# Attention and gated MLP on one core: pairs of neighbouring units by rows, a ring of six row buffers, output projections one iteration later

## The chip, the core and the metric

The kernel runs on one core of one Trainium2 chip. Such a core has a matrix engine (TensorE, "PE" in the profile, with its weight loads shown apart as "PEld"), a vector engine (VectorE, DVE), an engine for activation functions (ScalarE, ACT), a general engine (GpSimd, POOL) and a queue that mostly issues transfers (SyncE, SP). Sixteen DMA engines serve all queues. The metric is the device time of one execution in microseconds; the time of a version is the median of its runs.

## What is computed

A transformer block with modulation: layernorm and grouped attention with a cached K and V, then layernorm and a gated MLP that mixes along the sequence. There are 2048 rows of width 512, 32 query heads over 8 K/V heads (four query heads share one), 2048 keys and a head width of 128.

```python
def _A_ref(x, k_cache, v_cache, wq, wo):
    q = (x @ wq).reshape(B, Sq, Hq, Dh) ...          # 32 heads
    k, v = repeat of the 8 cached heads, 4 times
    scores = einsum('bhqd,bhkd->bhqk', q, k) * Dh ** (-0.5)
    p = softmax(scores)
    o = einsum('bhqk,bhkd->bhqd', p, v)
    return o.reshape(B, Sq, Hq * Dh) @ wo

def _B_ref(x, w_in, w_sp, b_sp, w_out):
    z = gelu(x @ w_in); z1 = z[..., :Fh]; z2 = layernorm(z[..., Fh:])
    g = einsum('ts,bsf->btf', w_sp, z2) + b_sp
    return (z1 * g) @ w_out

mod = silu(c) @ w_mod                                # sa, ca, ga, sb, cb, gb
h = layernorm(x) * (1 + ca) + sa;  x = x + ga * _A_ref(h, ...)
h = layernorm(x) * (1 + cb) + sb;  x = x + gb * _B_ref(h, ...)
```

## The kernel before

The attention is cut into 128 **units**. A unit is one of the 8 groups (a K/V head with its four query heads) and one of 16 tiles of 128 query rows; unit u belongs to group u // 16. One iteration of the main loop (L1350) computes the scores of unit `it` (`qk`, L986) and, beside them, the product with V of an earlier unit. It is cut into eight **slots**. A slot has two score products of 128x512 and one ScalarE instruction that takes the exponential of both (1024 columns), an eighth of a V product, and mostly one "fill": a step of the query projection for later units (L944; four per unit) or of the output projection (`wo_proj`, L1108; four per unit, in slots 4 to 7).

The order of all instructions is written out by hand: each engine executes its queue in the order in which the program issues, and waits where data or a buffer is missing. `at(it, slot, fn)` puts a step at the start of a slot; `later` and `fill` hold these steps. Loads by POOL's queue run as early as their buffers allow, in the queue's own order, since POOL has little else to do.

A unit is computed in one of two ways:

- **By columns.** The scores come transposed, keys on the partitions (L1020), the exponentials go straight into the buffer `pT` (L1027), and the product with V (`pv`, L1076) takes `pT` as the weights: 64 products of 129 columns, the 129th being the softmax sum. VectorE divides (L1087, L1088), and a DMA transpose on SyncE's queue turns the result into `oT` (L1096).
- **By rows.** The scores have queries on the partitions (L1001), the exponentials go to a row buffer `pn` together with their sums (L1008). `turn_rows` (L1034), two slots after a head is complete, divides the rows on VectorE (L1042) and issues a DMA transpose of 128x2048 into `pT` (L1045), so four per unit. The product with V (`pv_rows`, L1055) has V as the weights: 16 products of 512 columns. `oT` comes out as it is needed, and VectorE copies it (L1064).

`by_rows` (L967) chooses: even units from 8 to 120 go by rows (57 units), all others by columns. `pv_at` (L970) gives the iteration of the V product: u + 3 by rows, u + 1 by columns. The output projection follows two iterations later (L1359). `homes` (L974) hands out three `pT` buffers by when they come free. There are four row buffers, one for each head of a unit (L660): three lie in the tile for the MLP's input weights `win_sb`, and one in `wmod_a`, the first part of the modulation weights, both unused at that time.

The weights of the next group are loaded during a group: query weights `wq_g` at place 7, K at 9 (a DMA transpose from DRAM on SyncE's queue), V at 11, output weights `wo_g` at 13 (L1251 to L1256). `wq_g`, `v1` and `wo_g` have two buffers each and go by POOL's queue, so that a load starts when the last reader of the group before last is done. On the same queue are the layernorm's small operations and the rows `ga_rows` and `gb_rows`, which go out to DRAM and back at iteration 5 (`mod_rows`, L1171).

After the 128 units the MLP runs; its first part overlaps the last iterations, and it is not touched by the change.

Of the kernel before, what the change touches and what calls it, by code (L numbers as in the profile page):

```python
# [10 lines left out]
BF16 = mybir.dt.bfloat16  # L11
# [564 lines left out]
def kernel(  # L576
# [147 lines left out]
    def load_v(g):  # L724
        v1 = late.tile([P, NKT, DV], BF16, name="v1")
        nc.gpsimd.memset(v1[:, :, DH:DV], 1.0)
        if g > 0:
            nc.gpsimd.dma_start(out=v1[:, :, 0:DH], in_=v_dram[:, g])
        else:
            nc.sync.dma_start(out=v1[:, 0 : NKT // 2, 0:DH], in_=v_rows)  # L730
            nc.sync.dma_start(
                out=v1[:, NKT // 2 : NKT, 0:DH], in_=v_dram[:, 0, NKT // 2 : NKT]
            )
        groups[g]["v1"] = v1

# [230 lines left out]

    def by_rows(u):  # L967
        return TURN_A <= u < TURN_B and u % 2 == 0

    def pv_at(u):  # L970
        return u + 3 if by_rows(u) else u + 1


    users, homes = dict(pT0=-2, pT1=-1, wsp=CT + 2), {}  # L974
    for u in range(NU):
        homes[u] = min(users, key=lambda k: users[k])
        assert users[homes[u]] < u
        users[homes[u]] = pv_at(u)
# [7 lines left out]
    def qk(u, i):  # L986
# [10 lines left out]
        if by_rows(u):  # L997
            hh, half = divmod(i, 2)
            for c in range(2):
# [8 lines left out]
            nc.scalar.activation(  # L1008
                out=pn[hh][:, half * HK : (half + 1) * HK],
                in_=s_ps[:],  # L1010
# [21 lines left out]
        )  # L1032

    def turn_rows(u, hh):  # L1034
        c0 = u * REP + hh
        rs, rinv = rsums[u], rall[:, c0 : c0 + 1]
        tot = stat.tile([P, 1], FP32, name="tot")
        nc.vector.tensor_tensor(  # L1038
            out=tot[:], in0=rs[:, 2 * hh : 2 * hh + 1], in1=rs[:, 2 * hh + 1 : 2 * hh + 2], op=ALU.add
        )  # L1040
        nc.vector.reciprocal(out=rinv, in_=tot[:])  # L1041
        nc.vector.tensor_scalar(  # L1042
            out=pn[hh], in0=pn[hh], scalar1=rinv, scalar2=None, op0=ALU.mult
        )
        nc.sync.dma_start_transpose(  # L1045
            out=pTs[u][:, :, hh * P : (hh + 1) * P], in_=pn[hh]
        )

    def pv_rows(u, i, n):
# [12 lines left out]
        if i == n - 1:  # L1062
            oTs[u] = late.tile([P, REP, P], BF16, name="oT", bufs=3)
            nc.vector.tensor_copy(  # L1064
                out=oTs[u][:], in_=o_pss[u][:].rearrange("p (r q) -> p r q", r=REP)
            )

    def pv(u, i):
# [25 lines left out]
        if i == NSLOT - 1:  # L1094
            oTs[u] = late.tile([P, REP, P], BF16, name="oT", bufs=3)
            nc.sync.dma_start_transpose(  # L1096
# [253 lines left out]
    for it in range(NU + 6):  # L1350
# [202 lines left out]
```

## Time and profile before

| | |
|---|---|
| median of three runs | 1315.53 us (1315.16 to 1317.28) |
| the profiled execution's own time | 1315.63 us |
| its span, first to last instruction | 1313.5 us |
| PE busy | 1293.9 us, 99% |
| ACT busy | 1109.7 us, 84% |
| DVE busy | 683.1 us, 52% |
| transfers of SyncE's queue, share of 16 DMA engines' span | 62.3% |
| transfers of POOL's queue | 4.6% |
| V products by columns (L1076) | 4480 of 128x129 |
| V products by rows (L1055) | 912 weight loads of 128x128 |

Stages, by the view of stretches: up to 81.97 us the start and units 0 to 7, up to 116.14 the units 8 to 11 in which the rows begin, up to 1084.84 the alternating units, up to about 1130 the last units by columns, then the MLP to the end.

The busy times are sums over one profiled execution. Matmuls are pipelined and their ends are modelled, so a time per matmul is best read from the distance of two starts; in the timeline the length of one (0.38 us for 512 columns) is more than that distance. An entry in brackets after a line is idle time of the engine before that instruction, and what ended it.

### The profile page before, as it was taken

How to read it: one execution, taken by the hardware profiler on the slowest of the kernel's cores; microseconds unless marked ns; L12 is line 12 of the kernel's file. 1: busy time of each engine (PE TensorE's matmuls, PEld its weight loads, DVE VectorE, ACT ScalarE, POOL GpSimd, SP SyncE). 2: the span in 40 equal slices, each digit the busy share in tenths (PEclk: the TensorE clock that was granted, in tenths of full speed). 3: DMA queues.
4: the chain of work that ended last, by engine and by line, in shares of the span. 5: the costliest groups of instructions: out<-in, count | busy, mean ns of one | idle time of the engine just before them, and what ended most of it. 6: DMA issues, size and time to landing. Idle time of an engine off the chain costs nothing.

```text
span 1313.5 us, 24523 instructions
## 1 busy us (share of the span) xinstructions
PE 1293.9 (99%) x9452; PEld 740.6 (56%) x9623; DVE 683.1 (52%) x1675; ACT 1109.7 (84%) x1517; POOL 53.9 (4%) x96
## 2 busy tenths in 40 slices
PE   9999999999999999999999999999999999999998
PEld 5665555555555555555555555555555556644445
DVE  6644454444455544445454544444555686784444
ACT  7899999999999999999999999999999998650000
POOL 1110000000000000000000000000000011120000
PEclk9999999999999999999999999999999999999999
DMA  6479787978777777778786868687766673264300
GB/s 181 106 119 187 127 154 127 150 135 154 151 145 145 135 145 141 140 140 165 136 157 124 160 124 157 130 156 149 147 126 127 122 135 85 52 140 99 75 20 27
DMA packets 592172, 170.53 MB, mean 130 GB/s; under 512 B 581712, under 2 KB 588112, under 8 KB 592048
## 3 DMA queue, kind: packets, MB, share of 16 engines
q1 hardware_dynamic: 585024, 149.74, 62.3%
q0 software_dynamic: 4432, 16.91, 4.6%
q10 hardware_dynamic: 2592, 2.23, 0.5%
q8 instruction: 77, 1.26, 0.4%
q14 instruction: 47, 0.39, 0.1%
HBM read 21.89 MB, written 2.10 MB: 18 GB/s over the span
## 4 chain that ended last, share of the span: by engine, by line
PE 97%; DMA 1%; issue 1%; DVE 0%; ACT 0%; ACTq 0%; DVEq 0%
PE o_ps L1076 20%; PE s_ps L1020 19%; PE s_ps L1001 15%; PE o_ps L1055 15%; PE misc L1108 8%; PE misc L944 8%; PE misc L1433 7%; PE s_ps L1267 2%; PE s_ps L1306 2%; PE o_ps L1454 1%; DMA wsp<-wmod_a 1%; PE s_ps L1454 0%; DMA wmod_a<-in_w_mod_dram 0%; PE misc L854 0%; PE o_ps L785 0%
## 5 line engine op out<-in xcount | busy, mean ns | idle before, releaser
L1027 ACT ACTIVATE pT<-s_ps 128x1024 bf16<-128x1024 f32 x560 | 567.9, 1025 | 33.1 <-PE s_ps L1020 10.4
L1076 PEld LDWEIGHTS <-pT 128*128 128x128 bf16 x4480 | 299.5, 98 | 130.8
L1008 ACT ACTIVATE win_sb<-s_ps 128x1024 bf16<-128x1024 f32 x342 | 349.9, 1024 | 7.4 <-PE s_ps L1001 1.1
L1076 PE MATMUL o_ps<-v,pT 128*128 128x129 bf16 x4480 | 344.9, 220 | 1.2
L1020 PE MATMUL s_ps<-qT,kT 128*128 128x512 bf16 x1136 | 337.8, 379 | 2.9 <-ACT wmod_a L1008 1.3
L1001 PE MATMUL s_ps<-kT,qT 128*128 128x512 bf16 x889 | 266.5, 379 | 3.0
L1108 PE MATMUL misc<-wo_g,oT 128*128 128x512 bf16 x465 | 176.5, 380 | 1.7 <-DMA oT<-onorm 1.1
L1020 PEld LDWEIGHTS <-kT 128*128 128x128 bf16 x1136 | 110.1, 98 | 115.9 <-issue 4.5
L944 PE MATMUL misc<-hT,wq_g 128*128 128x512 bf16 (+2 forms) x480 | 172.7, 371 | 0.8
L1055 PEld LDWEIGHTS <-v 128*128 128x128 bf16 x912 | 89.2, 98 | 107.6
L955 DVE CAST qT<-misc 128x512 bf16<-128x512 f32 x125 | 85.7, 686 | 120.7 <-PE misc L944 120.6
L1064 DVE CAST oT<-o_ps 128x512 bf16<-128x512 f32 x57 | 39.4, 692 | 191.7 <-PE o_ps L1055 154.6
L1055 PE MATMUL o_ps<-wsp,v 128*128 128x512 bf16 x442 | 132.7, 379 | 0.6
L1042 DVE TENSOR_SCALAR win_sb<-win_sb,rall 128x2048 bf16<-128x2048 bf16 x171 | 128.8, 753 | 6.2 <-DVE rall L1041 0.3
L1055 PE MATMUL o_ps<-pT,v 128*128 128x512 bf16 x426 | 128.6, 379 | 0.6
L1001 PEld LDWEIGHTS <-qT 128*128 128x128 bf16 x912 | 89.1, 98 | 60.1 <-issue 0.2
L1008 ACT ACTIVATE wmod_a<-s_ps 128x1024 bf16<-128x1024 f32 x114 | 116.6, 1023 | 2.6 <-DMA wsp<-wmod_a 1.3
L1038 DVE TENSOR_TENSOR tot<-rs 128x1 f32<-128x1 f32 x228 | 35.2, 154 | 132.8 <-ACT win_sb L1008 131.6
L1433 PE MATMUL misc<-wsp,z 128*128 128x512 bf16 (+2 forms) x554 | 100.4, 336 | 0.5 <-issue 0.2
L1433 PEld LDWEIGHTS <-z 128*128 128x128 bf16 x560 | 50.6, 98 | 48.5
L1121 DVE TENSOR_TENSOR xacc<-misc,xacc 128x512 f32<-128x512 f32 x112 | 76.2, 680 | 0.0
L944 PEld LDWEIGHTS <-wq_g 128*128 128x128 bf16 x528 | 50.4, 98 | 29.3 <-issue 0.4
(107 smaller groups left out, 734.5 us busy)
## 6 DMA issues: line engine op xcount, KB each, us to landing
wq_g<-in_A_wq_dram POOLq DMA_DIRECT2D x7, 512.0 KB, 6.3
v<-in_A_v_cache_dram POOLq DMA_DIRECT2D x7, 512.0 KB, 6.2
wo_g<-in_A_wo_dram POOLq DMA_DIRECT2D x7, 512.0 KB, 4.3
wsp<-in_w_mod_dram POOLq DMA_DIRECT2D x1, 2048.0 KB, 10.3
out_dram<-yout ACTq DMA_DIRECT2D x16, 128.0 KB, 1.7
win_sb<-in_B_w_in_dram POOLq DMA_DIRECT2D x1, 1792.0 KB, 7.9
x_sb<-in_A_x_dram SPq DMA_DIRECT2D x3, 512.0 KB, 5.7
wsp<-win_sb SPq DMA_TRANSPOSE x87, 4.4
```

What stands on the lines that cost most here:

```text
L944: nc.tensor.matmul(ps[0][:, o0 : o0 + n], lhsT=wqs[g][:, dt, hh * DH : (hh + 1) * DH], rhs=hTs[ch][:, dt, c0 : c0 + n], start=(dt == 0), s ...
L955: nc.vector.tensor_copy(out=dst, in_=src)
L1001: nc.tensor.matmul(s_ps[:, c * 512 : (c + 1) * 512], lhsT=qTs[b][:, hh, jj * P : (jj + 1) * P], rhs=groups[g]["kT"][:, k0 : k0 + 512], sta ...
L1008: nc.scalar.activation(out=pn[hh][:, half * HK : (half + 1) * HK], in_=s_ps[:], func=ACT.Exp, scale=inv_sqrt_dh, accum_out=rsums[u][:, i : ...
L1020: nc.tensor.matmul(s_ps[:, h * 512 : (h + 1) * 512].rearrange("p (r q) -> p r q", r=REP), lhsT=groups[g]["kT"][:, kt * P : (kt + 1) * P], ...
L1027: nc.scalar.activation(out=pTs[u][:, 2 * i : 2 * i + 2, :], in_=s_ps[:].rearrange("p (k q) -> p k q", k=2), func=ACT.Exp, scale=inv_sqrt_dh,)
L1042: nc.vector.tensor_scalar(out=pn[hh], in0=pn[hh], scalar1=rinv, scalar2=None, op0=ALU.mult)
L1055: nc.tensor.matmul(o_pss[u][:], lhsT=groups[g]["v1"][:, kt, 0:DH], rhs=pTs[u][:, kt, :], start=(kt == 0), stop=(kt == NKT - 1),)
L1076: nc.tensor.matmul(o_ps[:, hh % 2, 0 : DH + 1], lhsT=pTs[u][:, kt, hh * P : (hh + 1) * P], rhs=groups[g]["v1"][:, kt, 0 : DH + 1], start=( ...
L1108: nc.tensor.matmul(X_ps[:], lhsT=oTs[u][:, hh, :], rhs=groups[g]["wo"][:, hh, :], start=(hh == 0), stop=(hh == REP - 1),)
L1121: nc.vector.tensor_tensor(out=xaccs[j][:], in0=X_ps[:], in1=xaccs[j][:], op=ALU.add)
L1433: nc.tensor.matmul(g_ps[:, :n], lhsT=z2[:, st, f * P : (f + 1) * P], rhs=wsp[t][:, st, c0 : c0 + n], start=(st == 0), stop=(st == NT - 1 a ...
```

## The change

- **Which units go by rows.** The list `kinds` replaces `by_rows`. In groups 1 to 6 each group has two pairs of neighbours by rows: the units at places 4 and 5, and those at 13 and 14. Between them the kinds alternate. There are 63 units by rows instead of 57.
- **When the V products run.** A loop gives one V product to each iteration (two where needed after unit 122), in the order of their due times; where none is due, one by rows that is due in the next iteration is taken.
- **Row buffers.** Two more tiles `pn0`, `pn1` in the pool `early`; the heads of all units by rows take the six in turn (`rows_of`).
- **Output projections.** Three iterations after the V product for units 8 to 121, two for the others (`wo_at`). `oT` has five buffers instead of three.
- **Loads of group 1.** Query weights, V and output weights are issued at iteration 5, slot 2; those of later groups stay at their places. Because V and the output weights of a group may now be loaded before its K, the dictionary of a group is made by whichever comes first.

```diff
+    pn += [early.tile([P, SK], BF16, name=f"pn{k}", bufs=1) for k in range(2)]
...
-        groups[g] = dict(kT=kT)
+        groups.setdefault(g, {})["kT"] = kT
...
-    def by_rows(u):
-        return TURN_A <= u < TURN_B and u % 2 == 0
-
-    def pv_at(u):
-        return u + 3 if by_rows(u) else u + 1
+    kinds, pv_its = [False] * NU, {}
+    for u in range(TURN_A, TURN_B):
+
+        pair = NT <= u < NU - NT and u % NT in (5, 6, 13, 14) and not kinds[u - 2]
+        kinds[u] = not kinds[u - 1] or pair
+    by_rows, order = kinds.__getitem__, [(u + 3 if kinds[u] else u + 1, u) for u in range(NU)]
+    order.sort()
+    for it in range(1, NU + 2):
+
+        due = [u for t, u in order if t <= it]
+        if not due and it > TURN_A + 1:
+            due = [u for t, u in order if t <= it + 1 and kinds[u]]
+        for u in due[: 2 if it > TURN_B else 1]:
+            pv_its[u] = it
+            order = [o for o in order if o[1] != u]
+    assert len(pv_its) == NU
+    pv_at = pv_its.__getitem__
+
+    def wo_at(u):
+        return pv_at(u) + (3 if TURN_A <= u < TURN_B else 2)
...
-                out=pn[hh][:, half * HK : (half + 1) * HK],
+                out=rows_of(u, hh)[:, half * HK : (half + 1) * HK],
...
+    def rows_of(u, hh):
+        return pn[(sum(kinds[:u]) * REP + hh) % len(pn)][:, 0:SK]
...
-        nc.vector.tensor_scalar(
-            out=pn[hh], in0=pn[hh], scalar1=rinv, scalar2=None, op0=ALU.mult
-        )
-        nc.sync.dma_start_transpose(
-            out=pTs[u][:, :, hh * P : (hh + 1) * P], in_=pn[hh]
-        )
+        rows = rows_of(u, hh)
+        nc.vector.tensor_scalar(out=rows, in0=rows, scalar1=rinv, scalar2=None, op0=ALU.mult)
+        nc.sync.dma_start_transpose(out=pTs[u][:, :, hh * P : (hh + 1) * P], in_=rows)
...
-            oTs[u] = late.tile([P, REP, P], BF16, name="oT", bufs=3)
+            oTs[u] = late.tile([P, REP, P], BF16, name="oT", bufs=5)
...
-        at(it + 7, 4, lambda g=g: load_wq(g, nc.gpsimd))
         at(it + 9, 5, lambda g=g: load_k(g))
-        at(it + 11, 4, lambda g=g: load_v(g))
-        at(it + 13, 4, lambda g=g: load_wo(g, nc.gpsimd))
+        at(*((5, 2) if g == 1 else (it + 7, 4)), lambda g=g: load_wq(g, nc.gpsimd))
+        at(*((5, 2) if g == 1 else (it + 11, 4)), lambda g=g: load_v(g))
+        at(*((5, 2) if g == 1 else (it + 13, 4)), lambda g=g: load_wo(g, nc.gpsimd))
...
-        pvs = [u for u in (it - 5, it - 3, it - 1) if 0 <= u < NU and pv_at(u) == it]
-        wos = [u for u in (it - 7, it - 5, it - 3) if 0 <= u < NU and pv_at(u) + 2 == it]
+        pvs = [u for u in range(max(it - 4, 0), min(it, NU)) if pv_at(u) == it]
+        wos = [u for u in range(max(it - 8, 0), min(it - 2, NU)) if wo_at(u) == it]
```

More of the change, by code (lines that the diff above doesn't have):

```diff
@@ L733, in load_v @@
             )
-        groups[g]["v1"] = v1
+        groups.setdefault(g, {})["v1"] = v1
     def load_wo(g, engine):
@@ L965 @@
     TURN_A, TURN_B = 2 * CT, NU - CT - 2
-    def by_rows(u):
-        return TURN_A <= u < TURN_B and u % 2 == 0
-    def pv_at(u):
-        return u + 3 if by_rows(u) else u + 1
+    kinds, pv_its = [False] * NU, {}
[15 more added lines that the diff above has]
+        return pv_at(u) + (3 if TURN_A <= u < TURN_B else 2)
     users, homes = dict(pT0=-2, pT1=-1, wsp=CT + 2), {}
     for u in range(NU):
-        homes[u] = min(users, key=lambda k: users[k])
+        homes[u] = min(users, key=users.get)
         assert users[homes[u]] < u
@@ L1094, in pv @@
         if i == NSLOT - 1:
-            oTs[u] = late.tile([P, REP, P], BF16, name="oT", bufs=3)
+            oTs[u] = late.tile([P, REP, P], BF16, name="oT", bufs=5)
             nc.sync.dma_start_transpose(
```

## The prediction

> **What bounds the kernel now.** I read the page first, then the chain, then single iterations of the loop over units in the views by stretch and by time. TensorE never rests:
>
> ```profile
> span 1313.5 us, 24523 instructions
> PE 1293.9 (99%) x9452; PEld 740.6 (56%) x9623; DVE 683.1 (52%) x1675; ACT 1109.7 (84%) x1517; POOL 53.9 (4%) x96
> DMA  6479787978777777778786868687766673264300
> PE 97%; DMA 1%; issue 1%; DVE 0%; ACT 0%; ACTq 0%; DVEq 0%
> ```
>
> The chain of work is 97% PE, so the end is set by PE's instructions and by the few holes between them. One iteration holds the scores of one unit and the product with V of an earlier one. Two neighbours, by stretch:
>
> ```profile
> core 0: us, PE busy (x) PEld busy (x) DVE busy (x) ACT busy (x) POOL busy (x), PEclk, DMA share, GB/s
> 570.27:579.07 8.80, 8.75 (x88) 5.97 (x88) 5.62 (x15) 8.69 (x16) 0.00 (x0) 1.00 0.43 81
> 579.07:587.71 8.64, 8.59 (x40) 3.91 (x40) 2.88 (x8) 8.30 (x10) 0.00 (x0) 1.00 0.95 177
> ```
>
> In the first, unit 64's scores go by rows beside a V product by columns (64 products of 129 columns); in the second it is the other way round (V product by rows, 16 of 512). They repeat as 17.44 us from unit 12 to 120 with one exception. In the timeline a 512-column product starts every 0.216 us, eight 129-column ones take 0.453. So a V product costs 16 x 0.216 = 3.46 us by rows and 8 x 0.453 = 3.62 by columns; the difference is the 8.80 against 8.64.
>
> ScalarE looks as full, but follows PE. Where PE has gaps, ScalarE does a half head by rows each 1.00 us (eight: 8.0), under PE's 8.64:
>
> ```profile
> 83.61 1.01 ACT L1008 ACTIVATE win_sb<-s_ps 128x1024 bf16<-128x1024 f32 x1
> 84.61 1.02 ACT L1008 ACTIVATE win_sb<-s_ps 128x1024 bf16<-128x1024 f32 x1
> ```
>
> The holes on PE inside the loop are three:
>
> ```profile
> 104.27 0.39 PE L1108 MATMUL misc<-wo_g,oT 128*128 128x512 bf16 x1 [1.06 <-DMA oT<-onorm]
> 108.74 0.59 PE L1020 MATMUL s_ps<-qT,kT 128*128 128x512 bf16 x2 [0.78 <-ACT wmod_a L1008]
> 265.16 0.59 PE L1020 MATMUL s_ps<-qT,kT 128*128 128x512 bf16 x2 [0.54 <-ACT wmod_a L1008]
> ```
>
> **The margin that matters.** A unit by rows must be turned by four DMA transposes before its V product. For unit 64, whose scores start at 570.27, SyncE issues:
>
> ```profile
> 574.43 7.57 SPq L1045 DMA_TRANSPOSE wsp<-win_sb  x3
> 582.11 1.21 SPq L1096 DMA_TRANSPOSE oT<-onorm  x1
> 583.42 1.79 SPq L1045 DMA_TRANSPOSE wsp<-wmod_a  x1
> DMA to landing us min/median/max: 4.3/4.3/4.3
> ```
>
> The last line belongs to the fourth head: it lands 17.4 us after the unit's scores began. Over units 12 to 120 this is 17.2 to 18.3 for most. The V product starts at 26.68 (three iterations on): 9 us to spare. One iteration earlier it would start at 8.80 + 8.64 + 0.43 (two score products first) = 17.87, leaving about 0.4.
>
> The fourth landing is later when a weight load runs beside it. Unit 58 began at 517.95, its fourth transpose was issued at 531.04, and then:
>
> ```profile
> 531.54 0.75 POOL L720 DMA_DIRECT2D wq_g<-in_A_wq_dram  x1 [64.68 <-PE misc L944]
> DMA to landing us min/median/max: 6.5/6.5/6.5
> ```
>
> 6.5 instead of 4.3 (the lower line is the transpose's): landed at 19.62. Units 42, 74 and 90 show 20.27, 19.72, 19.26; unit 26 even 25.68, and that caused the hole at 265 (ring of four row buffers).
>
> **The Trainium skill.** "TensorE: Matmul & The Clock Gate", Back-to-back issue gap, gives N/2.4 + 2.5 ns: 216 for 512 and 56 for 129; the trace has 216 and 57. The same section's sustained 131 ns for N=512 is not seen here. "DMA: Bandwidth & Descriptors", Queues, rings and completion order, says each DMA engine goes round its queue rows packet by packet, and that a completion signal lands only after the engine's earlier writes on all queues. The late landings agree: a transpose's signal waits for a load that it doesn't use.
>
> **The change, part by part.** Sums are against the profiled execution's 1315.63 us (span 1313.5 and 2.13 around it), 0.10 over the median of 1315.53.
>
> 1. *Six more units by rows* (63 for 57, one per group 1 to 6). Six V products go from 3.62 to 3.46: 6 x 0.16 = -0.96. Scores cost PE the same 16 products. What it adds elsewhere is covered: ScalarE 8.0 against 8.64; DVE four normalisations of 0.75 and eight small ones, in an iteration with 5.62 busy of 8.80; four transposes, some 12 us of DMA engines. At a pair this makes eight transposes, about 24 us, in the three iterations (26 us) before the next unit by rows; the second unit's fourth lands at about 31 after the pair's start, and its product comes at 34.9. Without that cover PE would wait the excess.
>
> 2. *Weight loads of group 1* (query weights, V, output weights; 1.5 MB) move ahead of the modulation rows on POOL's queue, from 81.9-83.9 to about 60 us. Before, they ran through unit 8's transposes: its first head landed after 13.88 us (later units: 8.5 to 9.8), its fourth after 25.5. The first two holes follow from that. Without them iteration 10 would have four slots at ScalarE's 1.0 and four at 1.10, ending near 106.56 instead of 108.74: -2.2 (at worst 0). At 60 us they pass the last layernorm transposes (issued at 60.71, needed at 78.70) and ga/gb rows, needed in group 7: I take 0.
>
> 3. *Ring of six.* A row buffer is rewritten six heads later instead of four. The hole after unit 26, 0.70 with the pair's excess over 17.44, goes: -0.7 (0 if it recurs elsewhere).
>
> 4. *Output projections at +3* for units 8 to 121, with five oT buffers. The count stays, but iteration 12 has none and iteration 126 two. Slots without a fill go at 0.9 to 1.0 instead of 1.10: -0.6 at 12, and +0.8 at 126 (124 and the two-projection iteration 125 took 8.0 and 8.80). DVE in 125 and 126 has some 8.5 and 8.9 us of work, at the edge; two PSUM banks cover a lag of 4: 0. Sum +0.2.
>
> 5. *The order of V products.* One per iteration as before, but at each pair a product is pulled up. Working out the rule: units 20, 36, ... 100 (fourth of the group, first of its pair) and 29, 45, ... 109 get theirs two iterations on, not three. Everything behind it on PE waits, and ScalarE behind that. For 29 and its like nothing else loads then; against landings of 17.2 to 18.3 and a 0.1 release I take 0.05 each: +0.3.
>
> 6. *Where 4 meets 5.* The output weights' buffer comes free after the last projection of the group before last. That was iteration 19, and the load was issued 0.46 after iteration 20 began (186.36 for 185.90), before any transpose. By +3 it is iteration 20 itself, likewise 36, ... 100: the load is issued 8.80 + 0.47 = 9.27 us after the start of exactly the units whose product was pulled up, between third and fourth head. Unobstructed, such a load moves its data from 2.0 to 4.0 us after issue; here in the middle of full DMA engines. The delay of the fourth landing is not shown for this place. Lower bound 0, if the half-used stretch from 13 to 14.5 us takes it; upper 3, by unit 42. I take 1.5, the load's 2 us less part of that stretch. Landing 17.45 (mean of the six before) + 1.5 + 0.1 - 17.87 = 1.2 of wait, six times: **+7.1**. There is no slack to win it back, as PE is the bound.
>
> Sum: -0.96 - 2.2 - 0.7 + 0.2 + 0.3 + 7.1 = +3.7, so 1319.3, or 1319.2 by the median.
>
> **Rivals.** *The load fits in* (other side): if it delays the fourth head by under 0.3 us, no product waits, and the gains stand: -3.7 to -2.9, about 1312. For it: DMA share is 0.43 in one iteration of two. Against: the share is 0.95 in just the iteration concerned. It decides at a delay of 1.0: below it, no measurable loss. *Half of it*: delays of 0.4 to 1.0 give waits of 0.1 to 0.7, together 0.6 to 4; with the gains, 1313 to 1317, no change. *The load and transposes break each other up* as at unit 26: 8 us late once or twice, 6 more each: 1325 to 1332. For it: one of the five loads there did. *ScalarE becomes the bound in rows-beside-rows iterations*: 8.0 against 8.64 excludes it; even at 8.8 part 1 would only lose 0.96. That the pairs don't arise is excluded: 63 units, counted by the rule.
>
> **How the numbers follow.** Full collision 0.52, half 0.22, fits in 0.16, break-up 0.10. About 0.2% (2.6 us) is what a measurement can tell. Full collision exceeds it but for a few per cent, with the break-up: slower 0.60; half and the edge: same 0.24; fits in: faster 0.16. The forecast is 1319.2; its own range is 1316.5 to 1323. The range for all, with gains up to 3 at the low end and a delay of 2.7 at all six at the high end, is 1312.4 to 1327.
>
> **What would show it.** V products of units 20, 36, 52, 68, 84 and 100 with idle time before them, ended by a transpose, about 1.2 us each, and an output-weights load issued some 9.3 us after those units' scores began. No wait, or under 0.3, at 29, 45 and on. 100 to 110 us without holes; rows-beside-rows iterations of 8.64. Wrong if those waits are absent, if the oT or layernorm transposes wait near 60 to 80, or if PE waits on DVE at iterations 125 to 127.

## The result, and the profile after

The changed kernel takes 1356.3 us (median of four executions, 1348.37 to 1360.48), the kernel before 1316.28 us in the same comparison: a ratio of 1.0297, with a 95% interval of 1.0249 to 1.0345. It is 3% slower; 1319.2 was predicted, with a range up to 1327. The profiled execution of the changed kernel is the shortest of its four: 1348.37 us, so 32.7 us over the profiled execution of before (1315.63). The other three are 8 to 12 us longer still. What follows accounts for the 32.7.

The page of the changed kernel, the same lines as were shown of before (span, TensorE's share, the DMA share in 40 slices, the chain of work by engine):

```profile
span 1346.6 us, 24026 instructions
PE 1310.0 (97%) x9335; PEld 729.6 (54%) x9335; DVE 705.4 (52%) x1729; ACT 1112.0 (83%) x1565; POOL 54.2 (4%) x96
DMA  6589787898989797988789897989887773264300
PE 93%; DMA 5%; issue 1%; DVE 0%; ACT 0%; ACTq 0%; DVEq 0%
```

PE was 97% of the chain and is 93%; DMA was 1% and is 5%, so the end now hangs on transfers in places (the chain follows a transfer back to its issue, so 5% is more than PE's idle time). The slices of DMA are a tenth or two fuller in many places, and name none. The waits of PE (time in all, how often, the longest) say where it stood:

```profile
PE o_ps L1071 <- DMA wsp<-wmod_a: 15.0, 3, 7.5
PE o_ps L1071 <- issue: 11.1, 3, 6.5
PE misc L1124 <- DMA oT<-onorm: 1.3, 1, 1.3
PE o_ps L1071 <- DMA wsp<-pn: 1.0, 1, 1.0
PE o_ps L1071 <- DMA pT<-pn: 0.8, 2, 0.4
```

L1071 is the V product by rows. The first two lines are six waits, 26.1 us in all, and they are the six that the prediction named: units 20, 36, ... 100, at place 4 of their group. The third is an output projection at iteration 7. The last two are three of the six products pulled up at place 13 (29, 45, ... 109).

The timeline of PE around the product of unit 36 (start, length, instruction, and in brackets the idle time before it):

```profile
344.54 0.59 PE L1036 MATMUL s_ps<-qT,kT 128*128 128x512 bf16 x2
351.66 1.01 PE L1071 MATMUL o_ps<-pT,v 128*128 128x512 bf16 x2 [6.53 <-issue]
352.89 1.06 PE L1036 MATMUL s_ps<-qT,kT 128*128 128x512 bf16 x2
```

Two products of 512 columns took 0.59 before the wait, and 1.01 and 1.06 after it. Single microseconds of the same stretch, with PEclk, DMA share and GB/s as the last three columns, say why:

```profile
346.00:347.00 1.00, 0.00 (x0) 0.00 (x0) 0.83 (x2) 0.20 (x1) 0.00 (x0) 1.00 1.21 84
348.00:349.00 1.00, 0.00 (x0) 0.00 (x0) 0.00 (x0) 0.00 (x0) 0.00 (x0) 0.50 1.75 37
353.00:354.00 1.00, 1.00 (x4) 0.35 (x3) 0.00 (x0) 0.01 (x1) 0.00 (x0) 0.50 1.09 208
355.00:356.00 1.00, 1.00 (x7) 0.42 (x5) 0.00 (x0) 0.71 (x2) 0.00 (x0) 1.00 1.08 191
```

PE's clock fell to half at 347.48, some 2.4 us after PE had gone idle (0.74 in the microsecond from 347, 0.50 from 348), and came back at 354.31, 2.7 us after the product had started. The Trainium skill describes this, in "TensorE: Matmul & The Clock Gate", HAM oscillation: idle gaps of more than about 3.4 us halve the clock, and PE then starts cold. This trace agrees in kind, but less idle time was enough. In all the traces here the clock changes only on a grid of 3.41 us, which runs on through the whole execution, and a step at half clock goes with the idle time of PE in the step before it. The four steps around this wait:

```profile
344.07:347.48 3.41, 1.06 (x5) 0.29 (x3) 2.49 (x6) 2.13 (x5) 0.00 (x0) 1.00 1.25 87
347.48:350.89 3.41, 0.00 (x0) 0.00 (x0) 0.00 (x0) 0.00 (x0) 0.00 (x0) 0.50 1.36 168
350.89:354.31 3.42, 2.65 (x7) 1.02 (x8) 0.00 (x0) 0.32 (x1) 0.00 (x0) 0.50 1.14 218
354.31:357.72 3.41, 3.41 (x18) 1.51 (x17) 0.69 (x1) 3.01 (x4) 0.00 (x0) 1.00 1.14 213
```

The first number after the length is PE's busy time: PE was idle for 69% of the first step, and the next one ran at half clock. In the attention loops of the changed kernel and the twelve experiments, all 13 steps with 61% or more of idle time were followed by one at half clock, and none with 54% or less; of two at 60%, one was. The GB/s column has the other half of the story: the DMA engines show as busy as ever (1.21, 1.75) while they move 84 and 37 GB/s, against 208 when nothing but transposes runs.

The load beside that unit, from the timeline of POOL's queue, and its time from issue to landing:

```profile
336.37 0.76 POOL L739 DMA_DIRECT2D wo_g<-in_A_wo_dram  x1 [25.01 <-PE misc L1124]
DMA to landing us min/median/max: 12.9/12.9/12.9
```

The unit's fourth transpose, from the timeline of SyncE's queue, likewise:

```profile
340.98 8.54 SPq L1063 DMA_TRANSPOSE pT<-wmod_a  x1
DMA to landing us min/median/max: 10.6/10.6/10.6
```

Unit 36's scores began at 327.10, so the load is issued 9.27 us later, just as worked out. It lands after 12.9 us and the transpose after 10.6, at 351.58; the product starts 0.08 later. The transpose in flight when the load came was the third, issued 0.7 us ahead of it: it took 13.8 us, and the fourth landed 2.1 us behind it. A product that waits for nothing starts 17.87 us after its unit's scores began; the third column says how much later than that each of the six started, and that is what "late" means for products below. All six:

| unit | load, us to landing | product late by | its iteration (u + 2) longer than 8.63 by |
|---|---|---|---|
| 20 | 5.7 | 2.7 | 2.7 |
| 36 | 12.9 | 6.7 | 8.0 |
| 52 | 10.9 | 5.0 | 6.7 |
| 68 | 5.4 | 2.0 | 2.0 |
| 84 | 13.9 | 7.7 | 9.2 |
| 100 | 7.7 | 2.9 | 4.2 |
| sum | | 27.0 | 32.9 |

The waits view has 26.1 for the 27.0, as it counts from the modelled end of the matmul before. The difference of the two sums, 5.9 us, is work at half clock after the waits; it is in four of the six, 1.3 to 1.7 us each, and not in the two shortest waits.

The rest of the ledger, as distances of iteration starts: iterations 6 and 7 +1.5; 8 to 11 -2.3; 12 -0.5; 126 +0.8; the six pulled products of place 13 +2.4; the six more V products by rows -1.0; the hole after unit 26 -0.7. With 32.9 that is 33.1, the difference of the two spans (1346.6 and 1313.5).

### The profile page after: what moved, and what is told of

The parts are those of the page before. It is cut to its first block, busy times and chain, and to the rows that moved or that the text cites. A ratio compares the mean times of both kernels' runs of the same rounds, so it can differ in the third digit from the quotient of the medians.

```text
span 1346.6 us, 24026 instructions
## 1 busy us (share of the span) xinstructions
PE 1310.0 (97%) x9335; PEld 729.6 (54%) x9335; DVE 705.4 (52%) x1729; ACT 1112.0 (83%) x1565; POOL 54.2 (4%) x96
## 4 chain that ended last, share of the span: by engine, by line
PE 93%; DMA 5%; issue 1%; DVE 0%; ACT 0%; ACTq 0%; DVEq 0%
PE o_ps L1092 17%; PE s_ps L1036 16%; PE o_ps L1071 16%; PE s_ps L1017 15%; PE misc L945 8%; PE misc L1124 8%; PE misc L1449 7%; DMA wsp<-wmod_a 2%; PE s_ps L1283 2%; PE s_ps L1322 2%; PE o_ps L1470 1%; DMA pT<-win_sb 1%; DMA oT<-onorm 1%; DMA pT<-pn 1%; PE o_ps L786 1%
## 5 line engine op out<-in xcount | busy, mean ns | idle before, releaser
L1043 ACT ACTIVATE pT<-s_ps 128x1024 bf16<-128x1024 f32 x440 | 446.4, 1026 | 64.1 <-PE s_ps L1036 46.7
L1017 PE MATMUL s_ps<-kT,qT 128*128 128x512 bf16 x1008 | 299.8, 379 | 0.0
L1092 PEld LDWEIGHTS <-pT 128*128 128x128 bf16 x3520 | 235.3, 98 | 102.5
L1092 PE MATMUL o_ps<-v,pT 128*128 128x129 bf16 x3520 | 270.7, 220 | 0.0
L1024 ACT ACTIVATE win_sb<-s_ps 128x1024 bf16<-128x1024 f32 x252 | 258.0, 1025 | 3.3 <-ACT pn L1024 0.3
L1071 PE MATMUL o_ps<-pT,v 128*128 128x512 bf16 x592 | 177.5, 382 | 11.9 <-issue 11.1
L1071 PEld LDWEIGHTS <-v 128*128 128x128 bf16 x1008 | 98.5, 98 | 150.3 <-issue 34.7
L1024 ACT ACTIVATE pn<-s_ps 128x1024 bf16<-128x1024 f32 x168 | 172.0, 1025 | 2.1 <-ACT pn L1024 0.6
L1071 PE MATMUL o_ps<-wsp,v 128*128 128x512 bf16 x416 | 124.6, 383 | 16.0 <-DMA wsp<-wmod_a 15.0
L1062 DVE TENSOR_SCALAR win_sb<-win_sb,rall 128x2048 bf16<-128x2048 bf16 x126 | 94.9, 753 | 5.1 <-DVE rall L1060 0.8
L1024 ACT ACTIVATE wmod_a<-s_ps 128x1024 bf16<-128x1024 f32 x84 | 86.1, 1024 | 0.0
L1043 ACT ACTIVATE wsp<-s_ps 128x1024 bf16<-128x1024 f32 x80 | 81.9, 1024 | 4.9 <-PE s_ps L1036 1.2
```

What stands on the lines that cost most here:

```text
L1017: nc.tensor.matmul(s_ps[:, c * 512 : (c + 1) * 512], lhsT=qTs[b][:, hh, jj * P : (jj + 1) * P], rhs=groups[g]["kT"][:, k0 : k0 + 512], sta ...
L1024: nc.scalar.activation(out=rows_of(u, hh)[:, half * HK : (half + 1) * HK], in_=s_ps[:], func=ACT.Exp, scale=inv_sqrt_dh, accum_out=rsums[u ...
L1043: nc.scalar.activation(out=pTs[u][:, 2 * i : 2 * i + 2, :], in_=s_ps[:].rearrange("p (k q) -> p k q", k=2), func=ACT.Exp, scale=inv_sqrt_dh,)
L1062: nc.vector.tensor_scalar(out=rows, in0=rows, scalar1=rinv, scalar2=None, op0=ALU.mult)
L1071: nc.tensor.matmul(o_pss[u][:], lhsT=groups[g]["v1"][:, kt, 0:DH], rhs=pTs[u][:, kt, :], start=(kt == 0), stop=(kt == NKT - 1),)
L1092: nc.tensor.matmul(o_ps[:, hh % 2, 0 : DH + 1], lhsT=pTs[u][:, kt, hh * P : (hh + 1) * P], rhs=groups[g]["v1"][:, kt, 0 : DH + 1], start=( ...
```

## The experiments

The theory (A where an expectation uses the letter): the six waits come from the *meeting* of the output weights' load with the four transposes of a unit whose product has no slack, and from nothing else in the change. Rivals are that the pairs themselves cost the time (their exponentials, their eight transposes, the lack of slack alone), that the early loads of group 1 do, and that the load costs its own bytes wherever it stands. Each time below is the median of the kernel's executions, with their extremes and the ratio to the kernel before in the same session. In these sessions the kernel before had medians of 1318.35, 1315.90, 1315.89, 1315.84 and 1315.83, with single executions up to 1338.

### A third buffer for the output weights

```diff
-    pn += [early.tile(...) for k in range(2)]
+    pn += [early.tile(...) for k in range(1)]
...
-        wo_g = late.tile([P, REP, D], BF16, name="wo_g")
+        wo_g = late.tile([P, REP, D], BF16, name="wo_g", bufs=3)
```

The load no longer waits for the last projection of the group before last, so it runs a group's length earlier. Pairs, pulled products and later projections stay; one row buffer pays for the room.

> The changed kernel with three buffers for the output weights (and a ring of five row buffers, to make room), so that each group's load goes out right behind its V load at place 2 and not in the middle of the transposes of the unit at place 4. Theory A, the load among the transposes delays the pulled-up V product: the six waits at units 20, 36, ... 100 (33 us in the changed kernel's profile, slow clock behind them included) shrink to under 0.8 each, 1312 to 1320 us in all. Rival B, eight transposes of a pair in a row are too many, or the pull by itself is too early: the waits at place 4 stay above 2 us each, over 1330 us.

Measured: 1318.76 us (1316.13 to 1323.43), ratio 0.9984 (0.9952 to 1.0016). The products of place 4 are 0 to 0.44 us late, and the span of the profiled execution is 1315.2. Nearly all of the loss is gone with the load moved and one row buffer fewer.

### The output projection at +2 again

```diff
-        return pv_at(u) + (3 if TURN_A <= u < TURN_B else 2)
+        return pv_at(u) + 2
```

> The changed kernel with the output projection two iterations after the V product again, everything else kept. Theory A: the load then starts 0.5 us into iterations 20, 36, ... as in the kernel before, ahead of the first transpose; no wait over 0.8 at place 4; 1312 to 1320 us. Rival B: over 1330 us. Rival C, the later projection is needed to hide late oT transposes behind pairs: new waits on oT before the output projection, 1 us or more per pair, 1325 to 1345.

Measured: 1316.93 us (1314.97 to 1322.74), ratio 0.9983 (0.9958 to 1.0008). POOL's timeline of it, with the load beside unit 36 and its time to landing:

```profile
325.71 0.76 POOL L739 DMA_DIRECT2D wo_g<-in_A_wo_dram  x1 [16.20 <-PE misc L1124]
DMA to landing us min/median/max: 4.4/4.4/4.4
```

Unit 36 began at 325.25 here. Issued 0.5 us after that, before any transpose, the same load lands in 4.4 us instead of 12.9, and the unit's product is 0.18 late. So the later projection is one half of the collision. The next run shows the other half, the pulled product without slack.

### The later projection alone, on the kernel before

```diff
-            oTs[u] = late.tile([P, REP, P], BF16, name="oT", bufs=3)
+            oTs[u] = late.tile([P, REP, P], BF16, name="oT", bufs=5)
...
-        wos = [u for u in (it - 7, it - 5, it - 3) if 0 <= u < NU and pv_at(u) + 2 == it]
+        late_wo = lambda u: pv_at(u) + (3 if TURN_A <= u < TURN_B else 2)
+        wos = [u for u in range(max(it - 8, 0), min(it - 2, NU)) if late_wo(u) == it]
```

No pairs, so every product by rows comes at u + 3 and has 9 us of slack.

> The kernel before with the later output projection and five oT buffers alone, no pairs, no pull, old loads, ring of four. Theory A: the load runs into the transposes of unit 20 and its like just as in the changed kernel, their fourth head lands 20 to 25 us after the unit's start instead of 17.4, but the V product comes at 26.7, so nothing waits for it; at most the ring of four row buffers costs about 1 us in some groups: 1315 to 1322. Rival C, the later projection costs by itself: over 1330.

Measured: 1327.26 us (1315.27 to 1334.33), ratio 1.0033 (0.9997 to 1.0069). That is above the 1315 to 1322 expected, though the kernel before spread as far in the same session (1314.54 to 1337.88), and the ratio does not tell the two apart. Place 4 behaved as the theory says: the loads landed 15 to 23 us after their unit began, and the fourth heads 19.3 to 26.2 us after it, where these units have 17.2 to 18.3 in the kernel before. So the delay comes without any pair. No product waited; PE lost 1.25 and 0.2 us at two of the six, where scores waited for a row buffer. But the profiled execution took 1330.53, and its loss is somewhere else. From its waits of PE:

```profile
PE s_ps L1001 <- ACT win_sb L1008: 11.5, 2, 7.5
```

POOL's queue in that place:

```profile
86.37 0.76 POOL L720 DMA_DIRECT2D wq_g<-in_A_wq_dram  x1
```

SyncE's queue in that place:

```profile
86.34 18.51 SPq L1045 DMA_TRANSPOSE wsp<-win_sb  x2
```

Unit 8's first transpose was issued 0.03 us ahead of the three loads of group 1, which then landed after 17 to 20 us, and the transpose after 20.5. The row buffers did not come free, ScalarE could not write, and iterations 10 and 11 took 31.92 us instead of 18.05. It is the same meeting at the place from which the change had moved these loads. In the profile of before the loads were issued from 81.86 to 83.90, 2 to 4 us ahead of that transpose (85.97), which landed after 9.9. Here the two modulation rows ahead of them on POOL's queue were late (the first was issued 1.8 us later, the second after a wait of 12.5 us instead of 10.2), and so they came 4.5 us later, beside the transpose. What made those rows late was not separated from the edit.

### The load on SyncE's queue, in line with the transposes

```diff
-        at(*((5, 2) if g == 1 else (it + 13, 4)), lambda g=g: load_wo(g, nc.gpsimd))
+        at(
+            *((5, 2) if g == 1 else (it + 5, 0)),
+            lambda g=g: load_wo(g, nc.gpsimd if g == 1 else nc.sync),
+        )
```

The same bytes, still between the third and the fourth transpose of the same units, but in one queue with them. Two more things differ: the load is issued 12.9 to 14.0 us after its unit began, not 9.27, and goes out in packets of 1024 bytes, not 4096.

> The changed kernel with the output weights of groups 2 to 7 issued on SyncE's queue, at the start of iteration 21, 37, ..., that is just ahead of the fourth transpose of unit 20, 36, ...: same bytes at the same time, but in one queue with the transposes. If the stretching (9 to 14 us for the load in three of six cases) comes from two queues taking turns on the DMA engines, the load takes its 2 us in order and the waits at place 4 are 1 to 3 us each, 1320 to 1332. If it comes from the load itself, they stay at 2 to 9 us, over 1340.

Measured: 1339.44 us (1332.39 to 1340.94), ratio 1.0138 (1.0077 to 1.0199). Its waits of PE at the product:

```profile
PE o_ps L1071 <- DMA pT<-wmod_a: 7.5, 3, 2.7
PE o_ps L1071 <- DMA wsp<-wmod_a: 4.1, 2, 2.7
PE o_ps L1071 <- issue: 3.1, 2, 2.5
```

The six products are late by 2.8, 2.7, 1.6, 2.5, 2.7 and 2.8: even, where the change had 2.0 to 7.7, and within the 1 to 3 expected. So in line the load costs about the 2 us in which, by the prediction, it moves its data when nothing is beside it. That the one queue alone does this isn't shown: in the kernel before, four of five loads of query weights in POOL's queue, issued 13.6 us after their unit began, delayed the fourth landing by 1.8 to 2.8 us as well. The total is above the 1320 to 1332 expected, as four of the six halved the clock: iterations 38, 70, 86 and 102 lose 1.6 to 1.7 us more than they waited. (In the one of unit 36 the clock is 1.00 for 2.4 us of idleness, then half until 3.2 us after the product began.) Iteration 7 lost 4.2 us as well (1.5 in the change), at a place that the edit doesn't touch.

### Half the load

```diff
-        engine.dma_start(out=wo_g[:], in_=wo_dram[:, g * REP : (g + 1) * REP, :])
+        n = P if g < 2 else P // 2
+        engine.dma_start(out=wo_g[0:n], in_=wo_dram[0:n, g * REP : (g + 1) * REP, :])
+        if g >= 2:
+            nc.gpsimd.memset(wo_g[n:P], 0.0)
```

> The changed kernel with only half of the output weights loaded in groups 2 to 7 (64 of 128 partitions; the others are set to zero, so that part of the output projection is left out). If transposes and load take turns by packets, half the packets make the waits at place 4 about half: 1 to 4 us each, 12 to 20 in all with the slow clock behind them, 1325 to 1337 us. If any overlap breaks the streams up whatever its size, they stay at 2 to 9 us, over 1340.

Measured: 1331.24 us (1324.67 to 1337.44), ratio 1.0104 (1.0085 to 1.0123). The profiled execution is the shortest (1324.67); its waits of PE at the product (L1074 here):

```profile
PE o_ps L1074 <- issue: 5.4, 3, 3.5
PE o_ps L1074 <- DMA wsp<-wmod_a: 3.0, 3, 1.5
```

The six products are late by 1.7, 3.7, 0.8, 1.2, 0.9 and 1.0: 9.3 us against 27.0 with the whole load. Half the packets cost a third of the wait, and none of the six halved the clock: the iterations are longer by just the waits. The one of 3.7 lies across two steps of the clock's grid:

```profile
341.66:345.07 3.41, 1.96 (x10) 0.69 (x7) 3.03 (x8) 3.02 (x5) 0.00 (x0) 1.00 1.33 139
345.07:348.48 3.41, 1.36 (x7) 0.68 (x8) 0.28 (x1) 0.09 (x1) 0.00 (x0) 1.00 1.20 248
```

PE was idle for 43% of the one and 60% of the other. In these two executions the waits grow faster than in proportion to what the load brings, and the medians say the same: over the version with the projection at +2 (1316.93), half the load costs 14.3 us and the whole 39.4.

### The early loads of group 1 alone

```diff
-        at(it + 7, 4, lambda g=g: load_wq(g, nc.gpsimd))
+        at(*((5, 2) if g == 1 else (it + 7, 4)), lambda g=g: load_wq(g, nc.gpsimd))
```

V and output weights likewise, on the kernel before.

> The kernel before with the loads of group 1 at iteration 5, slot 2, alone. Theory A (a load beside transposes stretches both): the loads no longer meet unit 8's transposes, the two holes near 104 and 108 us go (2.3 us), and with them the spread of the kernel before (up to 1338 in some executions[...]); but they meet the layernorm and oT transposes of iterations 5 to 7 (1.2 to 1.5 us wait at iteration 7). 1313 to 1316 us with a narrow spread. Rival D, the spread comes from elsewhere: some executions of this kernel are over 1325 us too.

Measured: 1314.90 us (1313.13 to 1320.15), ratio 0.9984 (0.9967 to 1.0002). Iterations 10 and 11 take 15.74 for 18.05, the whole gain of part 2; iterations 4 to 7 take 38.93 for 36.85, and the waits view names the cost:

```profile
PE misc L1108 <- DMA oT<-onorm: 1.9, 1, 1.9
```

The loads at 60 us stretch the layernorm's and oT's transposes there, and an output projection waits. Gain and cost nearly cancel. No execution is over 1320.2, where the kernel before reached 1335.2 in the same session.

### Early loads at iteration 4, with a ring of six

```diff
+    pn += [early.tile([P, SK], BF16, name=f"pn{k}", bufs=1) for k in range(2)]
...
+        at(*((4, 3) if g == 1 else (it + 7, 4)), lambda g=g: load_wq(g, nc.gpsimd))
```

The other two loads and the use of the ring (`rows_of`) likewise, on the kernel before.

> The kernel before with the loads of group 1 at iteration 4, slot 3, where no 128x2048 or layernorm transposes run, and with the ring of six; no pairs, projection at +2. Theory A: no holes near 104, 108 and 265 us and none at iteration 7: 1312 to 1314.5 us, narrow spread, faster than the kernel before and than the changed one. If the early loads meet something there too, 1314 to 1318.

Measured: 1317.01 us (1314.34 to 1320.29), ratio 0.9993 (0.9968 to 1.0019). The place in the program was not the time on the chip: POOL's queue had run ahead, and the loads were issued at 38.07, 39.08 and 40.24, into the layernorm transposes of iterations 4 and 5. Iterations 4 to 7 took 39.40 instead of 36.85. The ring of six did its part: group 1 (units 16 to 31) takes 139.52 in it, without the 0.70 us hole of before. One hole of 0.6 us is left, at iteration 93: the product of unit 90 waited for its transpose, in spite of a slack of 9 us. The query weights of the next group had been issued 0.08 us after that transpose.

### The change with both mended, first attempt

```diff
-        return pv_at(u) + (3 if TURN_A <= u < TURN_B else 2)
+        return pv_at(u) + 2
...
-        at(*((5, 2) if g == 1 else (it + 7, 4)), lambda g=g: load_wq(g, nc.gpsimd))
+        at(*((4, 3) if g == 1 else (it + 7, 4)), lambda g=g: load_wq(g, nc.gpsimd))
```

> The changed kernel with the projection at +2 and the loads of group 1 at iteration 4, slot 3. Theory A: the run with +2 alone minus its 1.2 us at iteration 7; the pairs save 6 x 0.16 = 1.0 and lose 0.1 to 1.4 at each pulled product (2 to 3 us together), so 1314 to 1317 us and 0.5 to 3 us above the kernel without pairs (early loads at iteration 4, ring of six). Rival E, the pairs gain once nothing collides: at or below that kernel.

Measured: 1319.42 us (1316.79 to 1321.88), ratio 1.0010 (0.9995 to 1.0026). That is above the 1314 to 1317 expected; the 2.4 us over the kernel without pairs are within the 0.5 to 3. The early loads ran ahead here too: iterations 4 to 7 take 37.40. The groups take 139.36 to 139.95, but the last of them 142.33: unit 100's product was 1.8 us late, though its output weights were loaded early. No load is beside its fourth transpose. In the two microseconds from 900 all DMA engines move 90 and 27 GB/s, and a packet of 16 KB of an instruction queue starts there; that it is the cause isn't shown.

### The early loads held until iteration 4, no pairs

```diff
+    gate = res.tile([P, NDT], FP32, name="gate")
+    at(4, 5, lambda: nc.gpsimd.tensor_copy(out=gate[:], in_=modc[:, 3 * NDT : 4 * NDT]))
...
-        at(it + 7, 4, lambda g=g: load_wq(g, nc.gpsimd))
+        at(*((4, 5) if g == 1 else (it + 7, 4)), lambda g=g: load_wq(g, nc.gpsimd))
```

On the kernel before, V and output weights likewise. The small copy reads a part of the modulation that VectorE makes at about 50 us, so POOL's queue can't run ahead of it.

> The kernel before with the loads of group 1 held back on POOL's queue by a small copy of the second modulation columns (ready in iteration 4), so that they run at 51 to 58 us, after the second layernorm chunk's transposes and before the third's; no pairs. Theory A: neither iterations 4 to 7 (36.9 us in the kernel before, 38.9 with the loads at iteration 5) nor 10 and 11 (18.0 before, 15.7 without the load) wait: 1312.5 to 1314.5 us, narrow spread, faster than the kernel before by 0.1 to 0.3%. If the loads still meet transposes, iterations 4 to 7 take over 38 us and the time is 1314 to 1317.

Measured: 1313.05 us (1312.42 to 1315.63), ratio 0.9970 (0.9956 to 0.9985): faster than both kernels. POOL's queue in its profile:

```profile
49.90 0.18 POOL L1252 COPY gate<-modc 128x4 f32<-128x4 f32 x1 [12.03 <-DVE modc L865]
50.03 0.85 POOL L720 DMA_DIRECT2D wq_g<-in_A_wq_dram  x1
```

The one long wait of PE in its loop:

```profile
PE s_ps L1020 <- ACT wmod_a L1008: 1.6, 1, 1.6
```

The loads land in 3.9, 6.2 and 7.2 us, and nothing waits for it: iterations 4 to 7 keep their 36.85, and 10 and 11 take 15.74. The whole of part 2's gain comes without its cost. The wait of 1.6 us is a row buffer of the ring of four after unit 26.

### The pairs without collisions

The change, with the projection at +2 and the loads held in the same way.

```diff
-        return pv_at(u) + (3 if TURN_A <= u < TURN_B else 2)
+        return pv_at(u) + 2
...
+    at(4, 5, lambda: nc.gpsimd.tensor_copy(out=gate[:], in_=modc[:, 3 * NDT : 4 * NDT]))
...
-        at(*((5, 2) if g == 1 else (it + 7, 4)), lambda g=g: load_wq(g, nc.gpsimd))
+        at(*((4, 5) if g == 1 else (it + 7, 4)), lambda g=g: load_wq(g, nc.gpsimd))
```

> The changed kernel (pairs, pulls, ring of six) with the projection at +2 and the loads of group 1 held back as in the run without pairs: nothing of the load collisions is left. Pairs save 0.16 each by the sum (1.0 in all), and groups 1 to 6 lost 0.1 to 2.8 each in the run with projection +2 and loads at iteration 4. Theory A: 1313.5 to 1316.5 us, at or above the 1313.05 of the same kernel without pairs. Rival E, pairs pay: under 1312.8.

Measured: 1315.08 us (1314.38 to 1317.54), ratio 0.9979 (0.9961 to 0.9998). All 40 us of the loss are gone with pairs, pulled products and ring in place: the theory holds. But the version without pairs is 2.0 us better. The waits at the product are now those of place 13:

```profile
PE o_ps L1071 <- DMA wsp<-pn: 1.0, 1, 1.0
PE o_ps L1071 <- DMA pT<-pn: 0.8, 2, 0.4
```

Iterations 31, 47, 63 and 111 are 2.6 us longer than 8.63 together; there is no load beside them. The fourth head of units 29, 45, 61 and 109 lands 18.0 to 18.9 us after the unit began, and the product would start at 17.87.

### The ring of six with the loads held, no pairs; and one pair in each group

```diff
-        pair = NT <= u < NU - NT and u % NT in (5, 6, 13, 14) and not kinds[u - 2]
+        pair = NT <= u < NU - NT and u % NT in (5, 6) and not kinds[u - 2]
```

The first of the two kernels is the one with held loads and no pairs, with the ring of six added. The second is the one above with this edit: 60 units by rows, and six pulled products (units 20, 37, 52, 69, 84, 101) instead of twelve.

> The kernel before with the group-1 loads held until iteration 4 and a ring of six row buffers, no pairs, output projections as before. If the ring is worth what part 3 of the prediction says, it closes the hole of 1.6 us at iteration 29 that the same kernel with a ring of four shows in its profile, and nothing else moves: every group from unit 16 to 112 takes 139.52 us, the time is 1311.8 to 1313.0 (the ring of four: 1313.05). If the hole comes from elsewhere than the row buffers, or the ring only matters in some executions, the median stays at 1313.05 within 0.4 while the spread narrows. A loss (over 1313.6) would speak for a cost of the two more buffers, which no theory here gives a reason for.

> The changed kernel with output projections two iterations after the product, group-1 loads held until iteration 4, and only the first pair in each group (60 units by rows; the pulled products are those of units 20, 37, 52, 69, 84, 101). If the pairs give nothing because the products pulled at place 13 wait (2.6 us in the version with both pairs), half the gain of the pairs is left here, 6 x 0.08 = 0.5 us, against waits of 0 to 0.3 us at six places (0.7 us together in that version): the same time as with the ring of six and no pairs, within 0.7 us, so 1312 to 1313.5, and some 1.5 to 2.5 us under the version with both pairs (1315.08). If the pairs cost something else, at their exponentials or transposes, the loss is about half of that version's loss: 1313.8 to 1314.5.

Measured: 1313.24 us (1312.24 to 1314.58), ratio 0.9979 (0.9971 to 0.9987) for the ring, and 1313.99 us (1313.47 to 1314.79), ratio 0.9985 (0.9979 to 0.9992) for one pair. With the ring every group takes 139.52, without a hole, but the median stays where it was (1313.05 with four). The hole at iteration 28 is one of some executions: in the profiles with a ring of four and the projection at +2 it was 0, 0.70 or 1.81 us. The expected gain in the median, 0.05 to 1.2 us, wasn't there.

With one pair the expectation put the pairs' cost at place 13, and was missed by 0.5 us; the time lies in the range of its rival. The exponentials cost nothing that shows: iterations with rows beside rows still take 8.63. The profile has waits at the products pulled up at the first pair too:

```profile
PE o_ps L1071 <- DMA pT<-win_sb: 0.8, 1, 0.8
PE o_ps L1071 <- DMA pT<-pn: 0.5, 1, 0.5
```

Iterations 54 and 103 are 0.6 and 0.9 us longer. Worked out over the six groups: they take 837.12 us with the ring and no pairs, 838.61 with one pair, 839.32 with two. Adding what their V products by rows save (3 x 0.16 and 6 x 0.16), the pulled products cost 2.0 us for six and 3.2 for twelve, 0.3 each on the average, against the 0.08 that each brings. It is not even: in the version with both pairs those of place 4 cost 0.1 each and those of place 13 0.4; with one pair, two of the six have 1.6 of the 2.0. Their fourth heads land 17.6 to 18.7 us after the unit began, where the ring of six without pairs has 17.2 to 17.7 at the units of place 4. Whether the eight transposes of a pair do that was not separated.

## Why the prediction was wrong

Direction and place were right, part by part, and so was the mechanism in outline: a load delays a landing, and a product without slack waits. The size was not.

- **Part 6, where 4 meets 5: the step that failed.** The load is issued where the prediction put it (9.26 to 9.28 us for 9.27), the six products wait as named, and moving the load removes the waits (the third buffer, the projection at +2), as does giving the products back their slack (the later projection alone). The term that failed is "I take 1.5, the load's 2 us less part of that stretch", with its upper bound of 3 by unit 42. At this place the fourth heads land 17.8 us after their unit's start with the load out of the way (the version with +2), and with it at 19.8 to 25.5: a delay of 2.0 to 7.7, mean 4.5. The reasoning took the DMA engines as a store of work, to which the load adds its own 2 us. In the run with one queue that is nearly so (1.6 to 2.8 us). In the change it isn't: in the microseconds from 341 to 348 of its trace 10 to 21 of the load's packets of 4096 bytes are started in each, and 56 to 170 of the transposes' of 256 bytes, where transposes alone have some 830 and a load alone up to 89. From 341 to 349, together they move some 90 GB/s in the mean, less than half of what transposes move alone.
- **A second term was left out.** PE's clock after a wait. A wait of 1.2 us is 35% of a step of 3.41 and would not have touched it; those of 2.9, 5.0, 6.7 and 7.7 did, at 1.3 to 1.7 us each, 5.9 in all. So part 6 was 32.9 us for 7.1.
- **The rival of transposes and load that break each other up** had it: "8 us late once or twice" was 5 to 8 late three times, and 2 to 3 late three times. Five loads beside transposes had been seen, four mild and one not, and that one was taken as the exception. But all five were loads of query weights issued 0.2 to 0.7 us after the fourth transpose of their unit (0.2 at unit 26, the bad one); the load of part 6 is issued 4.0 to 6.2 us before it, beside the third. The sample was not one of the case. Nor was its bad one an accident. In all the traces, 26 loads of query weights were issued just behind a fourth transpose whose landing is recorded: six were issued up to 0.23 us after it, and it landed 22.1 to 26.8 us after its unit began; twenty were issued 0.26 to 0.65 us after it, and it landed at 19.1 to 20.8. In a mild one (unit 58) the transpose's data packets are nearly all started before the load's, and only its last 4-byte packets come among them, which fits the prediction's signal that waits for a load. At unit 26, as in the change, the data packets of both run side by side for some 7 us.
- **"Fits in" and "half of it"** are excluded: no product was less than 2 us late.
- **Part 2** gained what it promised (-2.3 for -2.2). Its cost was put at nothing and is 1.5 us at iteration 7, in the way that was named as what would make it wrong: the oT transposes wait near 60 to 80. The early loads alone show it too (1.9), and holding them until 50 us removes it.
- **Part 5**, 0.3 for the pulled products of place 13, measured 2.4. A product that waits for nothing starts at 17.87, as worked out. The step that failed is to take the range of landings of the kernel before, 17.2 to 18.3, for these units, and 0.05 of wait from it: in the changed kernel three of the six products start only at 18.4 to 19.0, and the fourth head of the last of these units lands at 18.9, beyond that range.
- **Part 1** was right: rows beside rows take 8.63, and ScalarE did not bind. Part 1 and the pull of part 5 are one thing, though, and together lose.
- **Part 3** was right in the profiled execution (no hole after unit 26), and is worth nothing in the median. **Part 4** was right: -0.5 at iteration 12 for -0.6, +0.8 at 126.

What stays open: why three of the six meetings delayed the transposes by 5 to 8 us and three by 2 to 3, though all six loads were issued at the same place within 0.02 us. The distance to the third transpose doesn't sort them: issued 0.6 to 0.7 us after it, the load made products late by 2.9 as well as by 5.0 to 7.7. Open are also the further 8 to 12 us of the executions without a profile. They go with the load, as no execution with the third buffer or with the projection at +2 is over 1323.5; longer waits of the same kind would do, but no profile shows it.

## What to carry to other kernels

A step moved by one iteration moves the release of a buffer, and the load behind it, to another place; ask what stands in the DMA queues there, and whether what it meets still has slack. Price a meeting of a load and transposes in two queues by the worst landing that the trace shows for that meeting, not by the load's bytes, and add some 1.5 us for a slow clock where PE's wait can fill 60% of a step of 3.41 us: here waits of 2.0 us or less never halved the clock, those of 2.5 to 3.7 did or did not by where they fell, and those of 5.0 and more always did. A gain of 0.08 us an iteration isn't worth the last of a slack of 9 us: in the versions here the loads moved out of the way gave all there was to have (1313.05 for 1315.89), and the pairs cost 0.75 to 1.8 us on top of that.

## What was not expected of the hardware

- A load of 512 KB that lands in 4.4 us by itself took 5.4 to 13.9 us beside transposes of another queue, and a transpose that lands in 4.3 us took 10.6; from 343 to 349 us all DMA engines together moved 37 to 117 GB/s while shown as more than fully busy, where transposes alone move 208. The Trainium skill ("DMA: Bandwidth & Descriptors", Queues, rings and completion order) has each engine go round its queues packet by packet; the packets of both kinds side by side in the trace agree with that. Why the sum falls by more than half isn't shown.
- A tenth of a microsecond can decide: query weights issued up to 0.23 us after a fourth transpose let it land 22.1 to 26.8 us after its unit began, and 0.26 us or more after it 19.1 to 20.8.
- At the start of the rows the same meeting stretched a transpose to 20.5 us and three loads to 17 to 20 us, in a part that the edit of that run had not touched. The kernel before has these loads within 2 to 4 us of the same transpose. Its executions go up to 1338 us, where those with the loads held and no pairs stay under 1315.7, and no kernel with these loads moved and no meeting at place 4 is over 1323.5. But in the last session none of 33 executions of the kernel before was over 1318, and no long one was profiled, so the link is argued.
- PE's clock changed only on a grid of 3.41 us, and a step at half clock followed where PE had been idle for 61% or more of the one before, and never at 54% or less. So waits of 2.5, 2.7, 2.8 and 2.9 us halved the clock, and others of 2.7, 2.8 and 3.7 that lay across two steps did not.
